# Weight conversion, preparation and batch order of a two-stage attention and SoLU kernel re-planned

## The chip, the core and the metric

The kernel runs on one core of one Trainium2 chip. The metric is the device time of one execution in microseconds (us); lower is better. The core has five engines that run side by side, each through its own instructions in order: TensorE (PE in the rows, its weight loads PEld), VectorE (DVE), ScalarE (ACT), GpSimd (POOL) and SyncE (SP), which here issues every DMA.

## The reference, cut to what matters

```python
def _attn_ref(q, k, v, p):                 # q,k,v: (8, 8, 576, 64), p: (8, 8, 32, 64)
    def sm_attn(qq, kk, vv):
        s = scale * np.matmul(qq, kk.transpose(0, 1, 3, 2))
        s = s - np.max(s, axis=-1, keepdims=True)
        a = np.exp(s)
        a = a / (np.sum(a, axis=-1, keepdims=True) + 1e-09)
        return np.matmul(a, vv)
    p_packed = sm_attn(p, k, v)
    return sm_attn(q, p_packed, p_packed)

def _moe_ref(x, w_in, w_out, g_ln):        # x: 4608 x 512, w_in: 512 x 1024, w_out: 1024 x 512
    h = x @ w_in
    e = np.exp(h - np.max(h, axis=-1, keepdims=True))
    solu = h * e / (np.sum(e, axis=-1, keepdims=True) + 1e-09)
    mu = np.mean(solu, axis=-1, keepdims=True)
    var = np.mean((solu - mu) ** 2, axis=-1, keepdims=True)
    ln = (solu - mu) / np.sqrt(var + 1e-06) * g_ln
    return ln @ w_out
```

The attention's output, with batch and sequence as rows, is `x`. The three weights come in as 64-bit floats; everything else is 32-bit.

## The kernel before

**Preparation (batch 0 and the weights).** `w_in` and `w_out` arrive as pairs of 32-bit words in four chunks each, which one string, `LOADS`, puts between the loads of k, v, q and p. A chunk is converted in two steps: `high_part` (ACT L202, DVE L204 and L205) builds the upper bits, and `add_low_part` adds the lower word. The string `HOW` says for each of the eight chunks which engines do that second step: the lower word is scaled by ACT (L220) or inside one DVE instruction (L217), multiplied by DVE or GpSimd (L221), and added by DVE or GpSimd (L233) or by two matmuls and an ACT copy (L226, L227). For `w_out` there follow the column sums on TensorE (L302), one scale (L307 to L311), and for each of eight half chunks a multiplication by that scale (L322, `SCALED_BY`), a rounding to 16 bits `wch` (ACT L323) and the rest `wcl` (L330, `REST_BY`). `ZL_BY` and `A2L_BY` do the same for two tensors of batch 0.

**The attention of a batch b** is two generators. `pack(b)`: transposes of k (DVE L350), scores of p in two groups of matmuls (L368; L360 for batch 0), their maximum (L371, L373) and exponent (ACT L381), transposes (L397), the product with v (L407), `pp` (DVE L411) and its transpose (L413, L415). `unpack(b)`: transposes of q (L428), scores in two groups (L467), each read by DVE (L439), a softmax (DVE L443, GpSimd L444, ACT L446, DVE L448 to L450, GpSimd L451), `zh` and `zl`, the product of `w_in` with the packed values in two groups (matmuls L483, then ACT L485 and DVE L500), and `a2h` and `a2l` (L505, L507, L508). L368, L467, L483, L397 and L407 write the same two PSUM banks `pa`, so a group of 16 matmuls starts when VectorE or ScalarE has read both banks of the group before.

**The MLP** takes 36 tiles of 128 rows, called tile 0 to 35 here. `mlp_in`: 12 matmuls of 512 columns into `h` (L521; 24 for a tile that two batches share), the row maximum (DVE L523), exponent (ACT L531), the product `u` (DVE L534). `mlp_norm`: GpSimd's small `negmu` (L542), `yhl` in two halves (ACT L544, DVE L545), and one transposing DMA `yT` (L547, on SP's queue). `mlp_out`: 24 matmuls into `po` (L564), then DVE's `o_sb` (L566) and the store.

**What sets the order.** A scheduler places the instructions of each engine by priorities. The numbers in `PACK0`, `W_IN`, `UNPACK0`, `W_OUT`, `SCALE_AT`, `CHUNKS`, `PARTS` are priority offsets for the preparation; `FIRST_BATCH` and `LATER` say after which tile a step of `unpack(b + 1)` and of `pack(b + 2)` is written. From batch 1 on TensorE's order is that of the code. `BUSY` adds matmuls on constants that nothing reads (L255). SP takes its DMAs in one order, with at most eight under way.

## Time and profile before

| what | us |
|---|---|
| median of three runs | 471.25 (470.44 to 472.5) |
| the profiled execution's own time | 472.61 |
| its span, first to last instruction | 470.8 |
| TensorE busy in it | 430.8 (92%) |
| VectorE busy | 350.5 (74%) |
| ScalarE busy | 232.3 (49%) |
| GpSimd busy | 147.1 (31%) |

Times inside the profile count from the start of the span; the profiled execution is 1.8 us longer than its span, and 1.36 us above the median of the runs. The first output matmul (L564) starts at 108.85 us and the last ends with the span.

### The profile page before, as it was taken

The numbers are of one execution on the slowest core, as the hardware profiler recorded it, in microseconds if no ns is written. First come the engines' busy times: TensorE is split into PE (matmuls) and PEld (weight loads), VectorE is DVE, ScalarE is ACT, GpSimd is POOL, SyncE is SP. The second block draws the span as 40 slices with busy tenths as digits, with TensorE's granted clock in tenths as the row PEclk, the third lists the DMA queues.
The fourth block names the chain that finished last, engine by engine and source line by source line (L and its number), as shares of the span: only waits on it lengthen the run. The fifth ranks groups of instructions, "written<-read, shape, count | busy, mean of one in ns | idle before, by whom it ended". The sixth has DMA issues, their size and how long they took to land.

```text
span 470.8 us, 8265 instructions
## 1 busy us (share of the span) xinstructions
PE 430.8 (92%) x3116; PEld 234.4 (50%) x3116; DVE 350.5 (74%) x648; ACT 232.3 (49%) x404; POOL 147.1 (31%) x244
## 2 busy tenths in 40 slices
...
GB/s 257 338 274 290 149 205 118 130 208 148 104 151 173 165 120 202 159 140 137 220 71 165 98 206 101 98 100 173 51 84 68 92 45 90 112 67 130 73 101 77
DMA packets 237880, 67.00 MB, mean 142 GB/s; under 512 B 208912, under 2 KB 231440, under 8 KB 237328
## 3 DMA queue, kind: packets, MB, share of 16 engines
...
q8 instruction: 24, 0.39, 0.4%
...
## 4 chain that ended last, share of the span: by engine, by line
PE 42%; DVE 28%; POOL 7%; ACT 6%; issue 6%; DMA 6%; SPq 5%; DVEq 0%; ACTq 0%; POOLq 0%
PE po L564 21%; PE h L521 12%; DVE nm L523 4%; DMA zh<-in_moe_w_in_dram 3%; DVE u L534 3%; DVE qT L428 3%; DVE kT L350 3%; PE pa L407 3%; DVE yhl L545 2%; DVE zl L500 2%; ACT yhl L544 2%; SPq L134 2%; DMA raw<-in_k_dram 2%; ACT e L381 1%; DVE a2l L508 1%
## 5 line engine op out<-in xcount | busy, mean ns | idle before, releaser
L564 PE MATMUL po<-wch,yT 128*128 128x512 f16 x576 | 178.2, 380 | 1.2 <-DMA yT<-yhl 1.2
L564 PEld LDWEIGHTS <-yT 128*128 128x128 f16 x864 | 80.9, 98 | 113.0 <-issue 18.4
L564 PE MATMUL po<-wcl,yT 128*128 128x512 f16 x288 | 108.7, 379 | 0.0
L521 PE MATMUL h<-zh,a2h 128*128 128x512 f32 x160 | 69.3, 433 | 1.7 <-DVE u L534 1.7
L531 ACT ACTIVATE e<-h,nm 128x1024 f32<-128x1024 f32 x36 | 39.9, 1109 | 59.4 <-DVE nm L523 59.4
L544 ACT ACTIVATE yhl<-u,negmu 128x1024 f16<-128x1024 f32 x36 | 41.4, 1149 | 49.7 <-POOL negmu L542 49.2
L521 PE MATMUL h<-zh,a2l 128*128 128x512 f32 x160 | 64.6, 404 | 0.3 <-DVE a2l L508 0.3
L521 PE MATMUL h<-zl,a2h 128*128 128x512 f32 x160 | 63.9, 400 | 0.6 <-POOL zl L493 0.6
L523 DVE TENSOR_REDUCE nm<-h 128x1 f32<-128x1024 f32 x36 | 43.9, 1220 | 23.6 <-PE h L521 23.5
L545 DVE SCALAR_TENSOR_TENSOR yhl<-u,negmu,yhl 128x1024 f16<-128x1024 f32 x36 | 46.4, 1288 | 17.5 <-ACT yhl L544 17.3
L534 DVE SCALAR_TENSOR_TENSOR u<-e,s_row,h 128x1024 f32<-128x1024 f32 x36 | 45.6, 1267 | 8.6 <-ACT e L531 7.4
L551 POOL TENSOR_SCALAR s_eps<-se,s_row 128x1 f32<-128x1 f32 x36 | 10.8, 301 | 121.7 <-ACT e L531 80.5
L566 DVE SCALAR_TENSOR_TENSOR o_sb<-po,c_row,inv 128x512 f32<-128x512 f32 x36 | 26.6, 738 | 22.6 <-PE po L564 22.6
L549 ACT ACTIVATE e<-u,negmu 128x1024 f32<-128x1024 f32 x36 | 40.9, 1137 | 3.4 <-POOL negmu L542 3.4
L554 POOL TENSOR_SCALAR c_row<-sq,s_eps 128x1 f32<-128x1 f32 x36 | 17.7, 492 | 79.4 <-ACT e L549 79.3
L521 PEld LDWEIGHTS h<-zh,a2h 128*128 128x128 f32 x160 | 31.0, 193 | 16.5 <-issue 7.9
L521 PEld LDWEIGHTS h<-zh,a2l 128*128 128x128 f32 x160 | 30.8, 192 | 9.0 <-DVE a2l L508 1.3
L521 PEld LDWEIGHTS h<-zl,a2h 128*128 128x128 f32 x160 | 30.8, 193 | 7.1 <-POOL zl L493 0.9
L485 ACT CAST zh<-pa 128x512 fp32r<-128x512 f32 x28 | 15.1, 583 | 26.1 <-PE pa L483 26.1
L444 POOL TENSOR_TENSOR s<-s,mx 128x576 f32<-128x576 f32 x14 | 15.9, 1158 | 36.9 <-DVE mx L443 36.9
L381 ACT ACTIVATE e<-pa,nmx 128x288 f32<-128x288 f32 x28 | 13.8, 497 | 26.9 <-DVE nmx L373 26.9
L483 PE MATMUL pa<-w_in_sb,ppT 64*32 64x512 f32 x224 | 19.9, 631 | 2.6 <-DVE zl L500 2.6
...
## 6 DMA issues: line engine op xcount, KB each, us to landing
...
```

Source lines behind the costliest of these rows:

```text
L381: nc.scalar.activation(dst, src, AF.Exp, bias=nmx, accum_out=es[:, n:n + 1])
L483: nc.tensor.matmul(banks[r][32 * g:32 * g + 32, :], lhsT=ppT[rows, 32 * g:32 * g + 32], rhs=w_in_sb[rows, g, cols], start=True, stop=True)
L521: nc.tensor.matmul(h[:, 512 * n:512 * n + 512], lhsT=lhsT, rhs=z[:, r, 512 * n:512 * n + 512], start=t == 0, stop=t == len(terms) - 1)
L523: nc.vector.tensor_reduce(out=nm, in_=h, axis=AX.X, op=ALU.max, negate=True)
L531: nc.scalar.activation(e, h, AF.Exp, bias=nm, accum_out=se)
L534: nc.vector.scalar_tensor_tensor(out=u, in0=e, scalar=s_row, in1=h, op0=ALU.mult, op1=ALU.mult, accum_out=su)
L544: nc.scalar.activation(yhl[:, 0], u, AF.Identity, bias=negmu)
L545: nc.vector.scalar_tensor_tensor(out=yhl[:, 1], in0=u, scalar=negmu, in1=yhl[:, 0], op0=ALU.add, op1=ALU.subtract)
L549: nc.scalar.activation(e, u, AF.Square, bias=negmu, accum_out=sq)
L554: nc.gpsimd.tensor_scalar(out=c_row, in0=sq, scalar1=1.0 / DF, scalar2=s_eps, op0=ALU.mult, op1=ALU.add)
L564: nc.tensor.matmul(po, lhsT=yT[:, a, c], rhs=w[:, c], start=c == 0 and t == 0, stop=c == NFC - 1 and t == 2)
L566: nc.vector.scalar_tensor_tensor(out=o_sb, in0=po, scalar=c_row, in1=inv, op0=ALU.mult, op1=ALU.mult)
```

## The change

Five strings move parts of the conversion. `HOW`: the first chunk of `w_in` loses both its GpSimd instructions to VectorE; the first of `w_out` loses an ACT and a GpSimd instruction to one of VectorE; the last of `w_out` moves its addition from GpSimd to VectorE. `SCALED_BY`: one half chunk goes from GpSimd to VectorE, two more from ACT and GpSimd to one fused VectorE instruction each. `REST_BY`: two go from GpSimd to VectorE, one the other way. `ZL_BY`: one of four goes to VectorE, which reads PSUM, without the ACT copy. `A2L_BY`: one of two goes from VectorE to GpSimd. `BUSY` drops from 22 to 6 matmuls. All priority offsets and both tables of batch orders have other numbers, and `LOADS` other places for k and one w. The two new strings `YT_BY` and `STORE_BY` are all 's', which leaves the DMAs on SP.

```diff
-HOW = '14313324'
-SCALED_BY = 'pppppdpp'
-REST_BY = 'pdddppdd'
-ZL_BY = 'pppp'
-A2L_BY = 'dd'
-PACK0 = [-350, 400, 2010, 365, -1000, 60, -2800, 200, 200]
...
-LOADS = 'wpkwvwwqooPoo'
-BUSY = [[8, 100], [6, 0], [0, -3000], [0, -100], [2, -190], [0, -485], [4, 200], [2, -2885], [28, 285], [134, -20], [26, 20], [64, 50]]
...
+HOW = '54316325'
+SCALED_BY = 'pppdpdss'
+REST_BY = 'pdddddpd'
+ZL_BY = 'pppd'
+A2L_BY = 'pd'
+PACK0 = [1025, -200, 100, 100, -160, -75, -75, 80, -50]
...
+LOADS = 'wkpwwvwqoooPo'
...
+BUSY = [[0, -3025], [0, -3000], [6, -400], [0, 850], [0, -20], [0, -10], [0, 100], [0, 400]]
+YT_BY = 'ssssssssss'
+STORE_BY = 's'
...
-        nc.sync.dma_start(yT.rearrange('p t c n -> p (t c) n'), yhl.rearrange('p t f -> p (t f)'), transpose=True)
+        queue = nc.scalar if YT_BY[min(row // P, 9)] == 'a' else nc.sync
+        queue.dma_start(yT.rearrange('p t c n -> p (t c) n'), yhl.rearrange('p t f -> p (t f)'), transpose=True)
...
-            nc.sync.dma_start(*stores.pop(0))
+            (nc.scalar if STORE_BY == 'a' else nc.sync).dma_start(*stores.pop(0))
```

Line numbers of the changed kernel are two to three higher (L523 for L521, L567 for L564). A row that is followed by "..." stands for itself and its like up to the next row shown.

**Place 1, the first batch.** SP's queue around the first transposes, before:

```order
L85 DMA raw_684<-in_q_dram 32x18x32 x16
L96 DMA raw_1353<-in_k_dram 32x72x32 x4
L85 DMA raw_1362<-in_q_dram 32x18x32 x11
L107 DMA v_sb_680<-in_v_dram 128x8x128 x2
L134 DMA v_sb_680<-in_v_dram 64x8x64
L547 DMA_TRANSPOSE yT_971<-yhl_968 128x16x128
L547 DMA_TRANSPOSE yT_1135<-yhl_1132 128x16x128
L85 DMA raw_1362<-in_q_dram 32x18x32 x5
L96 DMA raw_1860<-in_k_dram 32x72x32 x4
L547 DMA_TRANSPOSE yT_1225<-yhl_1222 128x16x128
```

and changed:

```order
L87 DMA raw_669<-in_q_dram 32x18x32 x16
L98 DMA raw_1332<-in_k_dram 32x72x32 x4
L87 DMA raw_1341<-in_q_dram 32x18x32 x11
L550 DMA_TRANSPOSE yT_1036<-yhl_1033 128x16x128
L109 DMA v_sb_665<-in_v_dram 128x8x128 x2
L136 DMA v_sb_665<-in_v_dram 64x8x64
L87 DMA raw_1341<-in_q_dram 32x18x32 x3
L550 DMA_TRANSPOSE yT_1085<-yhl_1082 128x16x128
L87 DMA raw_1341<-in_q_dram 32x18x32 x2
L550 DMA_TRANSPOSE yT_1204<-yhl_1201 128x16x128
```

The same loads stand ahead of the first transpose, except that the three DMAs of batch 2's v now follow it; the second and third transposes are spread between the q loads. TensorE at the same place, before (h_1174 is tile 3, h_1270 the shared tile 4, po_1145 and po_1236 the outputs of tiles 0 and 1, pa_896 to pa_935 batch 1's scores, pa_983 batch 1's first group of L483):

```order
L521 MATMUL h_1174<-zh_500,a2h0_182 128x512
...
L467 MATMUL pa_896<-qT_845,ppT_843 32x288
...
L467 MATMUL pa_934<-qT_845,ppT_843 32x288 x4
L467 MATMUL pa_935<-qT_845,ppT_843 32x288 x4
L521 MATMUL h_1270<-zh_500,a2h0_182 128x512
...
L483 MATMUL pa_983<-w_in_sb_126,ppT_843 32x512 x4
L483 MATMUL pa_984<-w_in_sb_126,ppT_843 32x512 x4
L564 MATMUL po_1145<-wch_127,yT_971 128x512
```

and changed (pa_832 is batch 2's first L368 group, h_1153 tile 3, h_1249 tile 4, po_1095, po_1215, po_1303 the outputs of tiles 0 to 2, pa_902 and pa_914 batch 1's scores, pa_948 to pa_963 its L483, pa_976 batch 2's second L368 group):

```order
L370 MATMUL pa_832<-kT_712,pT2_84 32x288 x4
L523 MATMUL h_1153<-zh_486,a2h0_182 128x512
...
L567 MATMUL po_1095<-wch_127,yT_1036 128x512
...
L523 MATMUL h_1249<-zh_486,a2h0_182 128x512
...
L469 MATMUL pa_902<-qT_851,ppT_828 32x288
...
L567 MATMUL po_1215<-wch_127,yT_1085 128x512
...
L469 MATMUL pa_914<-qT_851,ppT_828 32x288
...
L567 MATMUL po_1303<-wch_127,yT_1204 128x512
...
L485 MATMUL pa_948<-w_in_sb_126,ppT_828 32x512 x4
...
L485 MATMUL pa_962<-w_in_sb_126,ppT_828 32x512 x4
L523 MATMUL h_1249<-zh_946,a2h1_186 128x512
...
L370 MATMUL pa_976<-kT_712,pT2_84 32x288 x4
```

Batch 1's scores moved from ahead of the first output matmul to behind 15 of it, and the outputs of tiles 0 to 2 all stand ahead of batch 1's second L483 group; before, the third output stood behind it.

**Place 2, an even batch (batch 2; batches 4 and 6 are alike, 6 without L368).** TensorE before: pa_1893 scores, h_1937 and h_2036 tiles 9 and 10, pa_1965 and pa_2008 the two L483 groups, pa_2069 and pa_2135 the two L368 groups.

```order
L467 MATMUL pa_1893<-qT_1886,ppT_1841 32x288
...
L521 MATMUL h_1937<-zh_1456,a2h0_182 128x512
...
L483 MATMUL pa_1965<-w_in_sb_126,ppT_1841 32x512
...
L564 MATMUL po_1995<-wch_127,yT_1808 128x512
...
L483 MATMUL pa_2008<-w_in_sb_126,ppT_1841 32x512
...
L521 MATMUL h_2036<-zh_1456,a2h0_182 128x512
...
L368 MATMUL pa_2069<-kT_2062,pT2_84 32x288
...
L564 MATMUL po_2104<-wch_127,yT_1984 128x512
...
L368 MATMUL pa_2135<-kT_2062,pT2_84 32x288
```

and changed (h_1916, h_2001, h_2110 tiles 9 to 11; pa_1944 and pa_2061 L483's groups; pa_2091 and pa_2136 L368's):

```order
L523 MATMUL h_1916<-zh_1409,a2h0_182 128x512
...
L485 MATMUL pa_1944<-w_in_sb_126,ppT_1820 32x512
...
L567 MATMUL po_1974<-wch_127,yT_1787 128x512
...
L523 MATMUL h_2001<-zh_1409,a2h0_182 128x512
...
L567 MATMUL po_2048<-wch_127,yT_1963 128x512
...
L485 MATMUL pa_2061<-w_in_sb_126,ppT_1820 32x512
...
L370 MATMUL pa_2091<-kT_2027,pT2_84 32x288
...
L523 MATMUL h_2110<-zh_1409,a2h0_182 128x512
...
L370 MATMUL pa_2136<-kT_2027,pT2_84 32x288
```

Between the two L483 groups there were 12 output matmuls, now 36 and a tile; between the second of them and the first L368 group there were 12 and a tile, now 12 alone; between the two L368 groups there were 24, now one tile (12 matmuls of L521).

**Place 3, an odd batch (batch 3; 5 is alike).** TensorE before: pa_2553 and pa_2610 L483's groups, h_2624 tile 15, po_2675 the output ahead of L368's first group pa_2690, h_2723 tile 16.

```order
L483 MATMUL pa_2553<-w_in_sb_126,ppT_2348 32x512
...
L564 MATMUL po_2583<-wch_127,yT_2407 128x512
...
L483 MATMUL pa_2610<-w_in_sb_126,ppT_2348 32x512
...
L521 MATMUL h_2624<-zh_1963,a2h1_186 128x512
...
L564 MATMUL po_2675<-wch_127,yT_2572 128x512
...
L368 MATMUL pa_2690<-kT_2654,pT2_84 32x288
```

and changed (h_2520 and h_2608 tiles 14 and 15):

```order
L485 MATMUL pa_2506<-w_in_sb_126,ppT_2327 32x512
...
L523 MATMUL h_2520<-zh_1942,a2h1_186 128x512
...
L485 MATMUL pa_2580<-w_in_sb_126,ppT_2327 32x512
...
L567 MATMUL po_2567<-wch_127,yT_2386 128x512
...
L523 MATMUL h_2608<-zh_1942,a2h1_186 128x512
...
L370 MATMUL pa_2636<-kT_2546,pT2_84 32x288
```

Tile 14 moved between the two L483 groups; the distance from the second to L368 is still one tile and 12 output matmuls. Batch 1 has the same new order as batch 3, but at its start the first L483 group stands directly behind the scores, ahead of tile 5; before, tile 5 stood between them.

## Rows read from the trace of the kernel before

**Rows 1.** The page: span, and busy time and instructions of each engine.

```profile
span 470.8 us, 8265 instructions
PE 430.8 (92%) x3116; PEld 234.4 (50%) x3116; DVE 350.5 (74%) x648; ACT 232.3 (49%) x404; POOL 147.1 (31%) x244
```

**Rows 2.** Busy time of the engines in stretches (from:to, length, busy of PE, PEld, DVE, ACT, POOL, granted clock, DMA share, GB/s); the first is a stretch of the preparation, the last row sums nine stretches from 57 to 467 us.

```profile
20.00:70.00 50.00, 39.32 (x290) 19.55 (x290) 40.70 (x61) 33.69 (x60) 24.14 (x11) 0.81 1.13 240
57.00:109.00 52.00, 38.81 (x298) 22.14 (x298) 42.87 (x74) 30.50 (x59) 32.88 (x34) 0.80 1.08 168
109.00:142.00 33.00, 29.90 (x261) 13.81 (x259) 23.73 (x48) 14.01 (x27) 8.53 (x12) 1.00 0.77 129
...
sum 410.00, PE 385.07 PEld 206.26 DVE 311.79 ACT 195.83 POOL 123.32; mean PE 42.79 PEld 22.92 DVE 34.64 ACT 21.76 POOL 13.70
```

**Rows 3.** Timeline of SP's DMA queue, preparation and first batch (start, duration of the issue, what).

```profile
70.69 11.66 SPq L85 DMA_DIRECT2D raw<-in_q_dram  x16
82.48 6.18 SPq L96 DMA_DIRECT2D raw<-in_k_dram  x4
89.19 8.45 SPq L85 DMA_DIRECT2D raw<-in_q_dram  x11
97.74 1.07 SPq L107 DMA_DIRECT2D v_sb<-in_v_dram  x2
...
100.13 5.83 SPq L547 DMA_TRANSPOSE yT<-yhl  x2
...
117.52 3.23 SPq L547 DMA_TRANSPOSE yT<-yhl  x1
```

**Rows 4.** DMA issues in the stretch 100.2 to 100.3: the first transpose, us from issue to landing.

```profile
yT<-yhl SPq DMA_TRANSPOSE x1, 6.0
```

**Rows 5.** Timeline of TensorE around the first output matmul (start, duration, what, in brackets the idle time before and what ended it).

```profile
96.96 0.72 PE L467 MATMUL pa<-qT,ppT 64*32 64x288 f32 x16
102.40 1.55 PE L467 MATMUL pa<-qT,ppT 64*32 64x288 f32 x16 [4.71 <-DVE s L439]
...
108.85 0.39 PE L564 MATMUL po<-wch,yT 128*128 128x512 f16 x1
```

**Rows 6.** Timeline of VectorE: the second half of tile 0's yhl, and of batch 1's unpack the last a2l.

```profile
90.27 1.29 DVE L545 SCALAR_TENSOR_TENSOR yhl<-u,negmu,yhl 128x1024 f16<-128x1024 f32 x1 [1.56 <-ACT yhl L544]
...
120.47 0.74 DVE L508 TENSOR_TENSOR a2l<-s,a2h 128x576 fp32r<-128x576 f32 x1
```

**Rows 7.** Timeline of TensorE, from pack(2)'s transposes to batch 2's first L483 group.

```profile
134.34 1.58 PE L397 MATMUL pa<-ident,e 128*128 128x128 f32 x8 [1.03 <-ACT e L381]
...
141.06 1.08 PE L467 MATMUL pa<-qT,ppT 64*32 64x288 f32 x16 [0.62 <-DVE s L439]
...
145.06 1.09 PE L483 MATMUL pa<-w_in_sb,ppT 64*32 64x512 f32 x16
```

**Rows 8.** Timeline of TensorE, groups of L483 and L368 in the later batches.

```profile
152.32 1.04 PE L483 MATMUL pa<-w_in_sb,ppT 64*32 64x512 f32 x2 [0.89 <-DVE zl L500]
153.58 1.09 PE L483 MATMUL pa<-w_in_sb,ppT 64*32 64x512 f32 x14 [0.22 <-DVE zl L500]
...
166.70 1.19 PE L368 MATMUL pa<-kT,pT 64*32 64x288 f32 x16 [0.40 <-ACT e L381]
...
193.30 1.68 PE L483 MATMUL pa<-w_in_sb,ppT 64*32 64x512 f32 x16
...
206.31 0.72 PE L368 MATMUL pa<-kT,pT 64*32 64x288 f32 x16
...
254.43 0.67 PE L368 MATMUL pa<-kT,pT 64*32 64x288 f32 x2
255.94 0.71 PE L368 MATMUL pa<-kT,pT 64*32 64x288 f32 x14 [0.84 <-DVE zl L500]
...
384.56 1.69 PE L483 MATMUL pa<-w_in_sb,ppT 64*32 64x512 f32 x16 [1.45 <-DVE zl L500]
```

**Rows 9.** Timeline of TensorE, VectorE and ScalarE in batch 2, from its first L368 group to the tile behind the second.

```profile
200.38 0.72 PE L368 MATMUL pa<-kT,pT 64*32 64x288 f32 x16
...
203.71 0.82 DVE L371 TENSOR_REDUCE mx<-pa 128x1 f32<-128x288 f32 x2
...
205.69 0.20 ACT L381 ACTIVATION_READ_ACCUMULATOR e<-pa,nmx 128x1 f32 x1
...
206.95 0.50 PE L521 MATMUL h<-zh,a2h 128*128 128x512 f32 x1
...
209.81 0.39 PE L564 MATMUL po<-wch,yT 128*128 128x512 f16 x1
```

**Rows 10.** GpSimd's groups up to 110 us (busy, mean ns), conversion lines.

```profile
L221 POOL TENSOR_TENSOR u<-u 128x1024 fp32r<-128x1024 f32 (+1 forms) x5 | 13.0, 2604 | 27.6 <-ACT u L220 17.2 <-DVE u L212 10.4
L322 POOL TENSOR_TENSOR yhl<-yhl,o_sb 128x512 f32<-128x512 f32 x4 | 6.4, 1629 | 0.1
```

**Rows 11.** Timelines of GpSimd and VectorE in the preparation.

```profile
18.94 1.22 DVE L221 TENSOR_TENSOR u<-u 128x1024 f32<-128x1024 f32 x1 [1.02 <-ACT u L220]
...
42.65 2.75 POOL L233 TENSOR_TENSOR w_in_sb<-w_in_sb,u 128x1024 f32<-128x1024 f32 x1
43.12 2.84 DVE L204 TENSOR_SCALAR e<-e 128x1024 int32<-128x1024 int32 x1
...
77.25 1.76 DVE L322 TENSOR_TENSOR yT<-yT,o_sb 128x512 f32<-128x512 f32 x1
```

16 lines of the change are left out of this document (8 added, 8 removed).

## The prediction

> **What bounds the kernel now.** I read the page's span and busy times first: TensorE is busy 430.8 of 470.8 us, 92% [rows 1]. A share over the whole span hides where the idle 40 us lie, so the next view was the busy time by stretches. The sum from 57 to 467 us leaves TensorE idle for 410.00 - 385.07 = 24.9 us. Of these 52.00 - 38.81 = 13.2 lie between 57 and 109, so only 11.7 lie in the 358 us after the first output matmul [rows 2]. From 109 us on TensorE is the bound, and a better order can win 11.7 us there at the very most, 2.5% of the time. Before 109 it waits for something else: VectorE, ScalarE and GpSimd are all partly idle there too, and the clock granted to TensorE is 0.80 of full [rows 2].
>
> The timeline of SP's queue tells what. Its DMA issues for q, k, q and v follow one another from 70.69 us to 98.8 with next to no gap: 70.69 + 11.66 = 82.35, then 82.48 + 6.18 = 88.66, then 89.19 + 8.45 = 97.64 [rows 3]. The first transpose (L547) is issued at 100.13, though the second half of its input, yhl, was ready at 90.27 + 1.29 = 91.56 [rows 6]. It lands 6.0 us after its issue [rows 4], about 106.1, and the first output matmul starts at 108.85 [rows 5]. So the preparation is bound by the stream of DMAs, not by the engines that convert weights. While it waits, TensorE has batch 1's scores, whose second group waits 4.71 us for VectorE; the first group ran in 0.72 us at 96.96, the second, the same 16 matmuls, in 1.55 at 102.40 [rows 5].
>
> In the later batches I measured each wait by the group of matmuls that holds it, as the time from the group's start to its end, idle time before it included, less what an undisturbed group takes: 1.09 us for L483 [rows 7], 0.72 for L368 at 206.31 [rows 8]. By that batch 1 loses 153.58 + 1.09 - 152.32 + 0.89 - 1.09 = 2.15 at L483 and 0.40 + 1.19 - 0.72 = 0.87 at L368; batch 2 loses 1.68 - 1.09 = 0.59 at L483; batch 3 loses 255.94 + 0.71 - 254.43 - 0.72 = 1.50 at L368; batch 6 loses 1.45 + 1.69 - 1.09 = 2.05 at L483 [rows 8]. I take batch 4 as 2 and batch 5 as 3.
>
> **The conversion.** GpSimd loses two L221 of 2.60 us [rows 10], two L233 of up to 2.75 [rows 11], four L322 or L330 of 1.63 [rows 10] and one L493 of the same width, and takes one a2l: some 17 us less by these rows. VectorE takes four instructions of 1024 columns at 1.22 us [rows 11], five of 512 at about 0.66 (the a2l of 576 columns takes 0.74 [rows 6], 0.74 x 512 / 576 = 0.66), and gives one a2l of 0.74: 4.9 + 3.3 - 0.7 = 7.4 us more. ScalarE gives some 3 us. I cost all of it at nothing. The cover is SP's stream, which the conversion does not feed; VectorE is idle for 50.00 - 40.70 = 9.3 us from 20 to 70 [rows 2], so 7.4 fit. Without the cover it could cost what does not fit. Upper bound: if VectorE's moved instructions all meet GpSimd as L322 did at 77.25, in 1.76 instead of 0.66 [rows 11], the nine cost 9.9 us more, 17.3 in all, of which 8.0 do not fit.
>
> Rows 11 show what such a meeting is: L204 took 2.84 us at 43.12, in the shadow of a GpSimd instruction that ran from 42.65 to 45.40, and ended 0.56 behind it. The Trainium skill, page "SBUF — State Buffer", section "Who interferes with whom", says why: VectorE and GpSimd share a pair of ports as an exclusive lock, a VectorE instruction with two SBUF inputs needs it too, and the order of issue decides who waits. The trace agrees with both cases. The rule speaks against the change, since the moved instructions have two SBUF inputs each; by it the term is up to the 8.0 us and not 0.
>
> The 16 fewer dummy matmuls I cost at 0, because TensorE waits for the stream there; if its clock fell in the gap, the cost would be some of what lies before 57 us, all ahead of the same stream.
>
> **The first batch.** The first transpose now stands ahead of v's three DMAs, so it issues at about 97.7, when the q loads are through, 2.4 earlier, and lands about 103.7. The output matmuls of tile 0 start there. But the shared tile 4 and batch 1's scores now stand behind 15 of them. An output matmul takes (206.31 - 201.10) / 24 = 0.217 us, one of a tile's twelve (209.81 - 206.95) / 12 = 0.238 [rows 8, 9]; 15 and 6 make 4.7 us at full clock, 9.4 at half, so the scores start at 108.4 to 113.1, and I take 109.5, 12.5 later than the 96.96 of before. From there to the last a2l it was 120.47 + 0.74 - 96.96 = 24.3 us [rows 5, 6]. The same again would end at 133.8; tile 4's rest and the transposes of pack(2) (L397) stand behind it, which gives L397 at about 136.5. On the other side, TensorE has the same work to do by L397 as before, and it idled 33.00 - 29.90 = 3.1 us from 109 to 142 [rows 2]. If no wait is left, L397 starts at 134.34 - 3.1 = 131.2. Before it was 134.34 [rows 7]. So the term is -3.1 to +2.2; I take 0, since the 24.3 hold the 4.71 us wait that need not return.
>
> Behind that, batch 1's first L483 group stands directly behind the scores instead of behind a tile. It waits for L439 to read both banks: a wait for one L439 was 0.62 [rows 7], so 0 to 1.3; I take 1.0, because nothing stands between. pp (L411) may queue behind a yhl half of 1.29 on VectorE [rows 6]: 0 to 1.3, I take 0.5.
>
> **The later batches.** In odd batches tile 14 moves between the two L483 groups. VectorE gets a tile's 2.9 us more to read the first group, so zl is through before L368: -1.5 in batch 3 and in batch 5. Batch 1 has the same order: -2.15 - 0.87 = -3.0. But its L368 group can wait for the exponent of the one before: from the maximum's start to the exponent's end are 205.89 - 203.71 = 2.18 us [rows 9], so 0 to 2.1, half taken, 1.05. In batch 6, 36 matmuls and a tile stand between the L483 groups where 12 stood: -2.05. Batches 2 and 4 get the same, -0.59 each. What is late next is their L368: the first group stands only 12 output matmuls (2.6 us) behind L483, the second only one tile (2.86) behind the first. The distance of 2.6 + 2.9 = 5.5 that the first had sufficed in batch 2, so it can be late by 0 to 2.9. For the second the nearest link is 201.10 to 205.89 = 4.8 us [rows 9], with other work of VectorE in it, and 2.18 at least: 0 to 1.9. I take 1.4 together for each of the two batches, 2.8, nearer the low ends, since VectorE has a tile less to do there. The tail keeps its order: 0.
>
> Sum: 0 + 1.0 + 0.5 - 3.0 + 1.05 - 1.2 + 2.8 - 3.0 - 2.05 = -3.9. The profiled execution's own time is 472.61 and becomes 468.7; it stood 1.36 above the median, 471.25, so against the median I forecast 467.3, 0.8% less.
>
> **The rivals.** (a) *The waits only move.* Each wait of TensorE for VectorE is a queue's, and VectorE's work after 109 is unchanged, so what is taken from L483 comes back at L368, as it could by the 2.9 and 1.9 us above: up to 2 x 4.8 = 9.6 against gains of 9.2. At the middle of that (4.8 for both batches, and the full 2.1 in batch 1) the sum is near -0.9, the time 470 to 471.5. For it: batch 3 loses at L368 although its L483 lost nothing [rows 8]. Against it: gaps of a tile remove real queueing.
> (b) *Slower: batch 1's unpack comes too late.* If the 24.3 us chain repeats whole and starts at half clock, from 113.1, the last a2l ends at 137.4 and L397 starts at about 140, +5.7; with half the later gains that ends at 474 to 476. It decides when that a2l ends later than about 130. For it: the start is 12.5 us later; against it: 72 output matmuls stand ready as cover.
> (c) *Slower by the ports.* The conversion's 8.0 us reach q's loads, whose start at 70.69 waits for buffers that VectorE frees, and all later work shifts: 467.3 + 8.0 = 475.3, and it decides from 6.3 on, where the time passes 473.6. For it: the 2.84 and 1.76 of rows 11. Against it: 17 us of GpSimd's instructions are gone, so meetings are fewer.
> (d) *Better:* the first batch becomes bound by work, 3.1 less, and L368 costs nothing in batches 2 and 4: 461 to 464.
>
> **How the numbers follow.** Forecast 0.40 (465 to 469), (a) 0.27, (b) 0.18, (c) 0.06, (d) 0.09. A measurement of this kernel tells about 0.5% from no change. Faster is forecast and (d), 0.49; same is (a), 0.27; slower (b) and (c), 0.24. The range leaves out the lower end of (d) and the upper of (b): 461.5 to 475. The likeliest case's own range is 465 to 469.
>
> **What would show it.** The first transpose issued near 97.7 and landing near 103.7; the first output matmul about 104 and L397 at 131 to 136.5; no idle time at L483 in batches 1, 2, 4 and 6, none at L368 in 3 and 5, and less than 2 us at L368 in 2 and 4. SP's q loads still at 70.7 and unbroken would show the conversion hidden. I am wrong if those loads start 2 us later or earlier, since then the stream was fed by the conversion after all, or if TensorE's idle time after 109 stays near 11.7.

## The result and the profile after

The changed kernel takes 473.75 us (median of 10 runs, 472.11 to 476.3) against 472.13 before (10 runs): a ratio of 1.0051, 95% interval 1.0029 to 1.0074. It is a little slower; I had forecast 0.8% faster. Run once more it gave 474.16 us and 1.0050 (1.0029 to 1.0072).

The page of the profiled execution after; its own time is 476.3 us:

```profile
span 474.5 us, 8233 instructions
PE 427.3 (90%) x3100; PEld 232.8 (49%) x3100; DVE 357.9 (75%) x656; ACT 228.4 (48%) x400; POOL 135.3 (29%) x236
```

VectorE is busy 7.4 us more than in [rows 1] and GpSimd 11.8 less: the conversion moved in the direction that the diff says. SP's queue at the first transposes, to be read against [rows 3] (start, duration of the issue, what):

```profile
72.01 11.13 SPq L87 DMA_DIRECT2D raw<-in_q_dram  x16
83.27 6.29 SPq L98 DMA_DIRECT2D raw<-in_k_dram  x4
90.09 8.54 SPq L87 DMA_DIRECT2D raw<-in_q_dram  x11
98.73 2.06 SPq L550 DMA_TRANSPOSE yT<-yhl  x1
```

The stream is as unbroken as before, and the first transpose goes out 1.4 us sooner. The busy time by stretches (as [rows 2]; the last two rows lie in the new trouble):

```profile
57.00:109.00 52.00, 38.83 (x278) 23.24 (x279) 44.79 (x77) 31.00 (x63) 29.08 (x30) 0.80 1.27 170
109.00:142.00 33.00, 27.83 (x258) 12.80 (x264) 24.53 (x48) 12.86 (x23) 6.93 (x11) 1.00 0.87 135
125.00:140.00 15.00, 11.33 (x144) 6.44 (x142) 12.47 (x25) 8.16 (x16) 2.45 (x5) 1.00 0.98 120
141.10:152.70 11.60, 9.96 (x61) 4.66 (x61) 8.23 (x16) 2.44 (x4) 2.63 (x3) 0.56 1.11 200
```

The same kind of rows of before, for the same two places:

```profile
125.00:140.00 15.00, 12.52 (x153) 6.47 (x156) 10.22 (x23) 6.00 (x12) 1.53 (x5) 1.00 0.59 124
140.00:152.00 12.00, 10.81 (x84) 4.94 (x68) 10.33 (x21) 3.75 (x7) 4.14 (x6) 1.00 0.92 167
```

From 109 to 142 us TensorE idles 5.2 us instead of 3.1, and from 141 to 153 it works hard, but at a granted clock of 0.56 (0.50, called half clock here, is the lower of its two levels); before, the clock was full there. The timeline of TensorE in between shows the waits (in brackets the idle time before and what ended it):

```profile
103.22 0.39 PE L567 MATMUL po<-wch,yT 128*128 128x512 f16 x1 [2.35 <-DMA yT<-yhl]
...
109.64 0.72 PE L469 MATMUL pa<-qT,ppT 64*32 64x288 f32 x16
...
128.52 0.50 PE L523 MATMUL h<-zh,a2h 128*128 128x512 f32 x1 [1.28 <-ACT a2h L509]
...
134.80 1.59 PE L399 MATMUL pa<-ident,e 128*128 128x128 f32 x8 [0.83 <-ACT e L383]
137.01 0.41 PE L399 MATMUL pa<-ident,e 128*64 128x128 f32 x2 [0.62 <-ACT e1T L400]
...
141.11 0.30 PE L415 MATMUL pa<-ident,pp 128*128 128x128 f32 x1 [1.89 <-DVE pp L413]
141.80 1.22 PE L469 MATMUL pa<-qT,ppT 64*32 64x288 f32 x16 [0.38 <-DVE ppT L417]
143.63 1.57 PE L469 MATMUL pa<-qT,ppT 64*32 64x288 f32 x16 [0.62 <-DVE s L441]
145.82 2.32 PE L485 MATMUL pa<-w_in_sb,ppT 64*32 64x512 f32 x16 [0.62 <-DVE s L441]
148.07 0.79 PE L523 MATMUL h<-zh,a2h 128*128 128x512 f32 x1
...
152.76 0.39 PE L567 MATMUL po<-wch,yT 128*128 128x512 f16 x1
```

Before, behind the first row of [rows 7]:

```profile
136.12 0.41 PE L397 MATMUL pa<-ident,e 128*64 128x128 f32 x2 [0.20 <-ACT e1T L398]
...
139.03 0.30 PE L413 MATMUL pa<-ident,pp 128*128 128x128 f32 x1 [0.69 <-DVE pp L411]
139.72 0.72 PE L467 MATMUL pa<-qT,ppT 64*32 64x288 f32 x16 [0.38 <-DVE ppT L415]
...
146.08 0.39 PE L564 MATMUL po<-wch,yT 128*128 128x512 f16 x1
```

(e1T is ScalarE's copy of the transposed exponent, ppT VectorE's of the transposed pp.) An L485 group now lasts 2.32 us where it took 1.09 [rows 7]. Tile 5's twelve matmuls fill 148.07 to 152.76, 4.7 us; before, from the end of the scores to L483, 2.9.

All kernels of this study have, but for the dummies of fill and fill2, the same work between two of pack's groups of transposes (L397, L399 after), so the starts of these groups cut the trace into comparable sections. Each number below is the difference of two such starts in one profiled execution; the first is the start of the first output matmul, the last runs to the end of the span. A section is named after the batch whose tiles lie in it; the attention in it is that of later batches. In batch 1's section the scores and the L485 groups are those of `unpack(2)` and the L370 groups those of `pack(3)`; some texts below call them batch 1's.

| kernel | first output | to pack(2) | to pack(3) | to pack(4) | to pack(5) | to pack(6) | to pack(7) | to the end |
|---|---|---|---|---|---|---|---|---|
| tiles of batch | | 0 | 1 | 2 | 3 | 4 | 5 | 6, 7 |
| before | 108.85 | 25.49 | 38.68 | 41.98 | 52.89 | 42.22 | 52.83 | 107.86 |
| changed | 103.22 | 31.58 | 41.66 | 43.35 | 51.83 | 46.16 | 50.98 | 105.72 |
| changed, again | 103.56 | 31.56 | 40.39 | 43.62 | 52.90 | 43.78 | 50.98 | 105.81 |
| conv_only | 102.14 | 43.47 | 43.21 | 42.26 | 52.86 | 42.23 | 52.90 | 107.93 |
| later_only | 106.12 | 26.16 | 38.99 | 43.36 | 53.35 | 44.03 | 50.98 | 105.81 |
| later_back | 102.81 | 32.08 | 42.42 | 41.99 | 52.87 | 42.21 | 52.92 | 108.00 |
| l485_behind | 101.97 | 30.87 | 44.43 | 43.36 | 51.89 | 43.70 | 50.98 | 106.00 |
| norm_first | 103.52 | 32.64 | 41.68 | 43.35 | 51.65 | 43.62 | 50.98 | 105.76 |
| fill | 103.53 | 31.58 | 44.47 | 44.14 | 53.50 | 43.64 | 50.99 | 105.75 |
| fill2 | 102.32 | 31.34 | 41.27 | 43.35 | 55.31 | 43.74 | 50.98 | 105.89 |
| pp_first | 104.62 | 32.24 | 41.48 | 43.51 | 51.64 | 43.98 | 50.98 | 105.75 |
| ppt_first | 103.98 | 31.99 | 40.88 | 43.36 | 51.92 | 44.13 | 50.98 | 105.76 |
| yhl_last | 103.31 | 31.58 | 42.03 | 43.63 | 51.98 | 43.74 | 50.98 | 105.75 |
| kt_later | 103.03 | 31.32 | 40.13 | 43.36 | 51.85 | 46.00 | 50.98 | 105.83 |
| scores_early | 102.81 | 41.99 | 43.77 | 43.65 | 51.71 | 43.97 | 50.98 | 105.72 |
| scores_early_even | 102.67 | 42.48 | 43.89 | 42.77 | 52.43 | 42.74 | 51.83 | 105.79 |
| even_back_pp | 103.52 | 31.43 | 42.81 | 42.63 | 52.37 | 42.82 | 51.81 | 105.81 |
| mixed | 107.40 | 26.03 | 39.07 | 42.46 | 52.36 | 43.15 | 51.47 | 105.76 |
| mixed_kt | 107.62 | 24.78 | 38.66 | 42.42 | 52.38 | 42.79 | 51.82 | 105.73 |

The first output matmul starts between 102.0 and 104.6 us in kernels with the changed preparation, between 106.1 and 108.9 with before's, so single executions differ by 2 us there; the sections of batches 5 and 6 repeat within 0.3 us for one order.

### The profile page after: what moved, and what is told of

It is laid out like the page before. It is cut to its first block, busy times and chain, and to the rows that moved or that the text cites. A ratio compares the mean times of both kernels' runs of the same rounds, so it can differ in the third digit from the quotient of the medians.

```text
span 474.5 us, 8233 instructions
## 1 busy us (share of the span) xinstructions
PE 427.3 (90%) x3100; PEld 232.8 (49%) x3100; DVE 357.9 (75%) x656; ACT 228.4 (48%) x400; POOL 135.3 (29%) x236
## 4 chain that ended last, share of the span: by engine, by line
PE 61%; DVE 19%; DMA 11%; SPq 3%; issue 3%; ACT 2%; POOL 0%; DVEq 0%; ACTq 0%
PE po L567 33%; PE h L523 19%; DMA yT<-yhl 3%; DMA raw<-in_k_dram 3%; DMA raw<-in_moe_w_out_dram 2%; PE pa L485 2%; DVE kT L352 2%; PE pa L409 2%; PE pa L469 2%; DMA zl<-in_moe_w_in_dram 2%; DVE yhl L547 2%; DVE u L536 2%; DVE nm L525 2%; PE pa L370 1%; PE pa L399 1%
## 5 line engine op out<-in xcount | busy, mean ns | idle before, releaser
L567 PE MATMUL po<-wch,yT 128*128 128x512 f16 x576 | 181.5, 385 | 5.6 <-DMA yT<-yhl 5.6
L567 PEld LDWEIGHTS <-yT 128*128 128x128 f16 x864 | 81.7, 99 | 119.4 <-issue 20.6
L567 PE MATMUL po<-wcl,yT 128*128 128x512 f16 x288 | 110.5, 384 | 0.0
L523 PE MATMUL h<-zh,a2h 128*128 128x512 f32 x160 | 70.5, 441 | 6.1 <-ACT a2h L509 3.6
L533 ACT ACTIVATE e<-h,nm 128x1024 f32<-128x1024 f32 x36 | 40.1, 1113 | 70.3 <-DVE nm L525 70.3
L523 PE MATMUL h<-zh,a2l 128*128 128x512 f32 x160 | 65.3, 408 | 0.2 <-DVE a2l L510 0.2
L523 PE MATMUL h<-zl,a2h 128*128 128x512 f32 x160 | 64.9, 406 | 0.0
L547 DVE SCALAR_TENSOR_TENSOR yhl<-u,negmu,yhl 128x1024 f16<-128x1024 f32 x36 | 47.9, 1332 | 16.3 <-ACT yhl L546 16.2
L557 POOL TENSOR_SCALAR c_row<-sq,s_eps 128x1 f32<-128x1 f32 x36 | 19.1, 532 | 86.6 <-ACT e L552 86.6
L523 PEld LDWEIGHTS h<-zh,a2h 128*128 128x128 f32 x160 | 31.5, 197 | 22.2 <-issue 6.6
L523 PEld LDWEIGHTS h<-zh,a2l 128*128 128x128 f32 x160 | 31.3, 196 | 9.3 <-DVE a2l L510 1.1
L523 PEld LDWEIGHTS h<-zl,a2h 128*128 128x128 f32 x160 | 31.5, 197 | 6.4 <-DVE zl L490 0.3
L446 POOL TENSOR_TENSOR s<-s,mx 128x576 f32<-128x576 f32 x14 | 16.0, 1158 | 31.3 <-DVE mx L445 31.3
L441 DVE STREAM_TRANSPOSE s<-pa 128x288 f32<-128x288 f32 x28 | 11.9, 462 | 13.7 <-PE pa L469 13.7
```

Source lines behind the costliest of these rows:

```text
L446: eng.tensor_tensor(out=s2[r], in0=s2[r], in1=mx.unsqueeze(2).broadcast_to([P, NB, J]), op=ALU.subtract)
L523: nc.tensor.matmul(h[:, 512 * n:512 * n + 512], lhsT=lhsT, rhs=z[:, r, 512 * n:512 * n + 512], start=t == 0, stop=t == len(terms) - 1)
L533: nc.scalar.activation(e, h, AF.Exp, bias=nm, accum_out=se)
L547: nc.vector.scalar_tensor_tensor(out=yhl[:, 1], in0=u, scalar=negmu, in1=yhl[:, 0], op0=ALU.add, op1=ALU.subtract)
L557: nc.gpsimd.tensor_scalar(out=c_row, in0=sq, scalar1=1.0 / DF, scalar2=s_eps, op0=ALU.mult, op1=ALU.add)
L567: nc.tensor.matmul(po, lhsT=yT[:, a, c], rhs=w[:, c], start=c == 0 and t == 0, stop=c == NFC - 1 and t == 2)
```

## Experiments

### One half of the change at a time

conv_only, the kernel before with the five conversion strings:

```diff
-HOW = '14313324'
+HOW = '54316325'
-SCALED_BY = 'pppppdpp'
+SCALED_BY = 'pppdpdss'
...
```

> The kernel before with the five conversion strings of the change alone; order tables, priority offsets, loads and dummies as before. Theory (the conversion hides behind SP's stream of loads, the loss is in the later order): same time as before within 0.3%, q's loads at 70.7 us start within 1 us of that. Rival (VectorE and GpSimd meet, the stream starts late): q's loads start 2 us later or more, and the time is 0.5 to 1.7% longer.

488.64 us, ratio 1.0363 (1.0338 to 1.0388). The stream was on time, q's loads at 71.28 us, so neither side had the mechanism. TensorE's timeline (same columns as above):

```profile
115.58 0.71 PE L467 MATMUL pa<-qT,ppT 64*32 64x288 f32 x16
...
127.98 2.52 PE L483 MATMUL pa<-w_in_sb,ppT 64*32 64x512 f32 x16 [4.13 <-DVE zl L500]
...
145.61 2.71 PE L397 MATMUL pa<-ident,e 128*128 128x128 f32 x10 [4.85 <-ACT e L381]
```

Eight instructions more on VectorE (656 against 648) make the scheduler place the whole first batch in another order under the old priorities: batch 1's scores run at 115.6 instead of 97 us, and pack(2) at 145.6. The other priorities of the change are therefore no part that could be left out; conversion and first batch are taken as one piece from here on. The reverse, before's conversion under the change's priorities, was not run.

later_only (before, with the change's `LATER`) and later_back (the change, with before's `LATER`) cut it into the two pieces that do come apart:

> The kernel before with the change's LATER table alone. Theory (the loss is in LATER, by L483 ahead of tile 5 and by transposes late in SP's queue): batch 1's first L483 group costs 1 to 6 us and batch 4 up to 4, against 8 us won at other groups, so between 1% faster and 0.5% slower, with the same rows as in the changed kernel at L483 and L368. Rival (the loss comes from the first batch, whose tile 4 ends just ahead of L397 and fills VectorE and ScalarE there): no loss at batch 1's first L483 group beyond 1 us, and the time is about 0.9% shorter.

> The changed kernel with the LATER table of before. Theory (first batch and conversion cost 0.5 us, L397 at 134.8): the time of before within 0.3%, and the waits of before at L483 and L368 are back. Rival (the first batch's order is what costs): TensorE still waits near 1.9 us for pp and runs at half clock behind L397, and the time stays 0.5% longer or more.

later_only: 471.37 us, ratio 0.9998 (0.9980 to 1.0015). later_back: 477.16 us, 1.0112 (1.0092 to 1.0133). later_only's theory held: the time lies in its range, batch 1's first L483 group brings a loss of some 3.6 us (below), batch 4's section takes 1.8 more, and batches 5 and 6 win 1.9 and 2.1. So `LATER` wins nothing under before's first batch, and 3 us under the changed one. later_back's theory fell; the piece of preparation and first batch costs: with before's `LATER` it takes 5.5 us by the medians, and in its profile 0.55 up to pack(2) and 3.7 in the next section (42.42 against 38.68). Its rival held: TensorE waits 1.89 us for pp there too, and the clock is at half behind it.

### Batch 1's section

l485_behind moves the first L485 group of that section behind tile 5:

```diff
-ui = [4, 0, 1, 0, ...]
+ui = [3, 1, 1, 0, ...]     # loop of batch 1 alone
```

> The changed kernel with batch 1's first L483 group (L485 here) written behind tile 5 instead of ahead of it, as before; nothing else. Theory (that place lets TensorE idle, and the idle time drops its clock to half for the next 11 us): the stretch from L399 to the end of tile 5 and that group, 18.0 us in the changed kernel, shrinks by 2 to 5 us, and the time by as much, to 0.2 to 0.6% under before. Rival (the clock falls already from the 1.9 us wait for pp ahead of it): it shrinks by less than 1.5 us, and the granted clock in it stays near 0.56.

476.95 us, 1.0127 (1.0097 to 1.0157), and the section grew to 44.43. The theory fell. The stretch that it named, 18.0 us in the changed kernel, took 16.65, so it shrank by 1.3 as the rival allowed. TensorE's clock was at 0.50 from 140 to 145 us all the same, and the second L485 group waited again, as before the change. Over the whole section the place ahead of tile 5 is the better one in the changed kernel.

What that place costs by itself is read from later_only, where the first batch is before's. The section is cut at the start of its scores and where tile 5 and the first L483 group are both done (us, one profile each):

| kernel | first batch | first L483 group | to the scores | to the end of both | rest |
|---|---|---|---|---|---|
| before | before's | behind tile 5 | 5.38 | 6.36 | 26.94 |
| mixed (below) | before's | behind tile 5 | 5.37 | 7.91 | 25.79 |
| later_only | before's | ahead of it | 5.38 | 9.93 | 23.68 |
| later_back | changed | behind tile 5 | 8.13 | 9.20 | 25.09 |
| l485_behind | changed | behind tile 5 | 8.13 | 8.52 | 27.78 |
| changed | changed | ahead of it | 7.00 | 10.96 | 23.70 |
| changed, again | changed | ahead of it | 6.95 | 9.38 | 24.06 |

In later_only the middle part is 3.57 us longer than before. The new wait is 0.57 of it; the rest comes with the half clock, at which the L483 group takes 2.25 us to the next start and tile 5 4.25:

```profile
141.09 2.32 PE L483 MATMUL pa<-w_in_sb,ppT 64*32 64x512 f32 x16 [0.57 <-DVE s L439]
143.34 0.79 PE L521 MATMUL h<-zh,a2h 128*128 128x512 f32 x1
...
147.59 0.39 PE L564 MATMUL po<-wch,yT 128*128 128x512 f16 x1
```

```profile
140.00:145.00 5.00, 4.43 (x30) 1.77 (x21) 4.45 (x8) 1.07 (x2) 0.25 (x1) 0.50 1.06 249
```

So the half clock does not need the changed first batch: the new place of this group is followed by it too, and with the changed first batch it comes at either place. What only the changed first batch brings, of these seven, is the 1.6 to 2.8 us more ahead of the scores. mixed has before's order in this section and yet 0.66 granted from 140 to 145, so single executions differ by some 1.5 us here.

The next three take tile 4's work, which now ends just ahead of pack(2)'s steps, from in front of them on VectorE. pp_first makes the second half of tile 4's yhl wait for pp, ppt_first for ppT, yhl_last for the transposes of the scores (L441):

```diff
+late = 0 * pp[:, 1, :1] + negmu                      # VectorE; ppT or the scores in the other two
-yhl[:, 1] = (u + negmu) - yhl[:, 0]
+yhl[:, 1] = (u + late) - yhl[:, 0]
```

> The changed kernel with one order turned on VectorE: pack(2)'s pp (L413) ahead of the second half of tile 4's yhl (L547), by a one-column instruction that makes yhl wait for pp; every other engine's order is the same. Theory (tile 4 ends just ahead of pack(2)'s last steps, its work on VectorE stands in front of pp, and the gap that this makes on TensorE brings the half clock): TensorE's wait for pp falls from 1.9 to about 0.7 us, and the section from pack(2)'s L399 to pack(3)'s shrinks by 1.2 us by the wait alone and by up to 3 with the clock, to 38.5 to 40 us. Rival (tile 4's work only changes place; the scores' transposes on VectorE set the pace): the section stays within 0.5 us of 40.4 to 41.7.

> As the run with pp ahead of yhl, with the second half of tile 4's yhl behind the copy of ppT as well; the other engines' orders are the changed kernel's. In the run with pp alone, the wait for pp fell by 1.2 us and the wait for ppT grew by 1.1, since yhl now stood ahead of that copy. Theory: both waits are short now, batch 1's scores start 1.2 us earlier after pack(2)'s L399 (5.8 instead of 7.0 us), and the section from pack(2)'s L399 to pack(3)'s shrinks by 1 to 3 us from 40.4 to 41.7. Rival: yhl now delays the transposes of the scores (L441), and the section stays.

> As the run above, with the second half of tile 4's yhl behind all the transposes of batch 1's scores, so that nothing of tile 4 stands on VectorE from pp to there. Theory: the section from pack(2)'s L399 to pack(3)'s falls to 38 to 39.5 us, near before's 38.7 to 39.1, and the time by 1 to 3 us against the changed kernel. Rival (ScalarE's copies behind tile 4's exponent, and the idle time ahead of L399, are enough to bring the half clock): the section stays above 40 us.

pp_first 474.6 us (1.0057, 1.0031 to 1.0082), ppt_first 473.24 (1.0017, 1.0000 to 1.0034), yhl_last 474.49 (1.0038, 1.0018 to 1.0058). In pp_first the wait only moved one instruction on, from pp to ppT:

```profile
141.96 0.30 PE L415 MATMUL pa<-ident,pp 128*128 128x128 f32 x1 [0.69 <-DVE pp L413]
143.72 1.22 PE L469 MATMUL pa<-qT,ppT 64*32 64x288 f32 x16 [1.46 <-DVE ppT L417]
```

In yhl_last both waits are short, and still the scores start 7.01 us behind L399 and the section takes 42.03 us: the clock falls already in L409, and an L486 group (L485 of the changed kernel) lasts 2.32 us, since the granted clock is at half:

```profile
141.07 0.45 PE L415 MATMUL pa<-ident,pp 128*128 128x128 f32 x1 [0.69 <-DVE pp L413]
141.90 1.22 PE L469 MATMUL pa<-qT,ppT 64*32 64x288 f32 x16 [0.38 <-DVE ppT L417]
...
145.93 2.32 PE L486 MATMUL pa<-w_in_sb,ppT 64*32 64x512 f32 x16 [0.62 <-DVE s L441]
```

```profile
138.00:151.00 13.00, 10.69 (x128) 5.09 (x121) 7.22 (x16) 3.57 (x6) 2.37 (x5) 0.50 0.93 168
```

So a shorter queue on VectorE behind L399 does not bring the clock back. ppt_first is the only one that may have won something, about 0.3%, at the edge of what its interval tells.

kt_later goes one step further up: pack(3)'s four k transposes (L352, 2.75 us) stand on VectorE between pack(2)'s maximum and nmx, before the change and after it; here they wait for nmx.

```diff
+kT[:, :, 0] = 0 * nmx of pack(2)                     # pack(3), ahead of its four transposes
```

> The changed kernel with pack(3)'s four k transposes (L352, 2.75 us on VectorE) put behind pack(2)'s nmx (L375) by a four-element write that they must wait for; in the changed kernel, and in before, they stand between pack(2)'s maximum and nmx, and nmx frees the exponent that L399 waits for. The scheduler then also places tile 4's exponent on ScalarE behind the e1T copies and its yhl behind ppT; TensorE's order is the changed kernel's. Theory (from batch 1's last a2l on, at 130.9 us, L399 follows VectorE's queue, and tile 4 collides with pack(2)): L399 comes up to 2.5 us sooner after the first output matmul (29 to 30 us instead of 31.6), less where tile 4's matmuls, which end at 134.0, are in its way (then 30.8); the section behind it shrinks by 1 us or more, and the time by 1 to 3 us. Rival (the half clock follows the idle time, wherever it stands): L399 comes sooner and the section behind it grows by as much.

474.0 us, 1.0035 (1.0018 to 1.0052). L399's wait of 0.83 us is gone, but tile 4's second half, behind its 1.28 us wait for a2h, ends only at 134.35; L399 starts 31.3 us behind the first output matmul, as in the changed kernel, and the clock is low on both sides of it (0.75 granted from 130 to 135 us, 0.50 from 140 to 145). What pp_first to kt_later have in common lies above L399: tile 4 waits for batch 1's a2h. As I read the trace, that is because batch 1's scores run at 109.6 and 115.1 us and not at 97 and 102.4 [rows 5], and the output matmuls of tiles 0 to 2, which lay beside that chain before, are used up ahead of it. No run shows that this brings the half clock: in later_only the same scores run at 94.81 and 100.26 us, and the clock falls in the section all the same.

scores_early was meant to put those scores back (`FIRST_BATCH`, first list: 0, 0, 5 becomes 0, 3, 2), and scores_early_even added before's even row:

> The changed kernel with one list of FIRST_BATCH other ([0, 0, 5, 0, ...] becomes [0, 3, 2, 0, ...]): batch 1's scores stand directly behind pack(1)'s ppT and behind tile 3, ahead of the first output matmul, as in before; preparation, conversion, LATER as in the change. Theory (batch 1's unpack starts 13 us late in the changed kernel, the output matmuls that could cover its chain are used up ahead of it, and from 125 us on TensorE waits and falls to half clock): the scores run near 97 us, batch 1's a2h is in time, the section from the first output matmul to pack(2)'s L399 shrinks by 1 to 3 us or the next one by 2, the clock stays full from 135 to 150 us, and the time is 2 to 5 us shorter, 469 to 472. Rival (the half clock comes from pack(2)'s own chain, exponent to pp): both sections stay within 1 us, and the time stays near 474.

> As the run above, with before's row of LATER for batches 2 and 4 besides. Theory: the sections of batches 2 and 4 are 0.7 to 1.3 us shorter each, batch 5's 0.8 longer, as in the run with that row before; 1 us less in sum. Rival: no difference.

488.48 us (1.0345, 1.0319 to 1.0372) and 487.58 (1.0336, 1.0312 to 1.0361). They decide nothing: the scores ran at 95.3 and 99.7, but the scheduler also put k's four loads ahead of two transposes in SP's queue; an output matmul waited 4.35 us for yT and L399 5.41 us for its exponent.

### The clock

fill and fill2 put dummy matmuls, which nothing reads, where TensorE waits in batch 1's section: ten (six) behind pack(2)'s L409 in unused columns of its bank, and six in a bank of the scores (three in a free bank) behind each group of scores.

> The changed kernel with 22 short dummy matmuls into unused columns of pa where TensorE waits ahead of batch 1: ten behind pack(2)'s L409, six behind each group of batch 1's scores (1.6 and 0.6 us of work at full clock). They compute nothing that is read. Theory (the half clock from 141 to 153 us is what idle TensorE brings, and it costs 3 to 4 of the 6.2 us lost there): the clock stays at full, and the section from pack(2)'s L399 to pack(3)'s shrinks from 41.7 to between 37.5 and 39.5, the time by 0.4 to 0.9%. Rival (the engines ahead are late, the clock follows): the section shrinks by less than 1 us, or grows by the dummies' time.

> As the run with 22 dummies, but fewer, and no longer in the banks that VectorE reads: six of 384 columns behind pack(2)'s L409, and three of 512 columns into a free po bank behind each group of batch 1's scores. Theory (clock): the granted clock stays at full from 135 to 155 us, tile 5's 12 matmuls take near 2.9 us instead of 4.7, and the section from pack(2)'s L399 to pack(3)'s takes 38 to 39.5 us instead of 40.4 to 41.7. Rival: the clock falls all the same, or the section does not shrink although the clock stays.

fill: 479.46 us, 1.0160 (1.0127 to 1.0192); fill2: 474.18, 1.0039 (1.0008 to 1.0069). Dummies in a bank wait for its reader, or it for them: in fill the six behind each group of scores stand 0.98 us for L441, and the group behind them with them, so its section grew by 3 us although the clock stayed full until 145. In fill2 pp stands 0.88 us for the six ahead of it, but behind the scores the clock is back (0.50 from 140 to 145 us, 0.91 from 145 to 150):

```profile
139.00 2.27 PE L411 MATMUL pa<-ones 128*128 128x384 f32 x6
141.93 0.45 PE L415 MATMUL pa<-ident,pp 128*128 128x128 f32 x1 [0.66 <-DVE pp L413]
...
147.19 1.27 PE L485 MATMUL pa<-w_in_sb,ppT 64*32 64x512 f32 x16
148.38 0.50 PE L523 MATMUL h<-zh,a2h 128*128 128x512 f32 x1
```

The L485 group and tile 5 take 1.2 and 2.9 us to the next start, where the changed kernel takes 2.25 and 4.69, 2.9 us more (in its second profile 2.25 and 3.33, 1.5 more). That is the price of the half clock in these two steps, measured at either level. The section as a whole, 41.27 us, won nothing: from L399 to the scores it took 9.10 us instead of 7.00. Half of that arose ahead of the dummies, where TensorE stood 2.09 us for ScalarE's e1T, and the rest at the dummies and behind them. So the price of the half clock is measured, but no run took it away and kept the rest.

### The later batches

after_again is the changed kernel once more; norm_first puts `mlp_norm` back to offset 1000 in `LATER`, which changes SP's queue alone: in the loops of batches 2 and 4 a transpose stands ahead of v's loads instead of behind them and q's.

> The changed kernel once more, for a second profile. If batch 4's 3.9 us more than before belong to this order of instructions, the section from L399 of pack(5) to that of pack(6) takes 46 us again; if they are an accident of one execution (its transposing DMA landed 0.04 us before the matmul that waited 2.1 us for it), it takes near 43.7, as in the two other kernels with the same LATER table. Batch 1's section stays at 41.7 and batches 5 and 6 at 51.0 and 105.8.

> The changed kernel with the priority offset of mlp_norm in LATER at 1000 as before; only SP's queue differs: in loops 2 and 4 a transpose stands ahead of v's loads instead of behind them. Theory (transposes behind v and q are a cost of the change in even batches): sections of batches 2 and 4 shrink by 0 to 2.2 us each, batch 4 more than batch 2, and the time by 0.2 to 0.6%. Rival (TensorE waits there for VectorE's readers of pa, L483 and L368, and the transposes are in time): same time within 0.2%.

after_again: 474.16 us (1.0050, 1.0029 to 1.0072), batch 4's section 43.78. So 2.4 us of the first profile's 46.16 were that execution's own. Its transpose was 2.09 us late, and the granted clock behind it was 0.70 (290 to 295 us); in the second profile the same wait was 1.39 us and the clock 1.00:

```profile
291.72 0.39 PE L567 MATMUL po<-wch,yT 128*128 128x512 f16 x1 [2.09 <-DMA yT<-yhl]
```

```profile
291.41 0.39 PE L567 MATMUL po<-wch,yT 128*128 128x512 f16 x1 [1.39 <-DMA yT<-yhl]
```

The transpose of that stretch is not late in one execution alone: in all eleven profiles with the change's row for batches 2 and 4 and its offset of `mlp_norm`, TensorE waits 1.1 to 2.1 us for a transpose in batch 2's or batch 4's section, and in four of them also in batch 3's (in after_again 1.10 us at 237.74, in fill2 1.97, in a section of 55.31). norm_first: 473.89 us, 1.0043 (1.0026 to 1.0059): against 1.0050 no difference that can be told. Its transposes in these two sections are in time, but L370 waits 0.90 and 0.93 us there for VectorE's zl, and the sections keep their length (43.35 and 43.62): the wait only changes its place.

mixed takes from the change only the rows of `LATER` for the loops of batches 3, 5 and 6; mixed_kt adds the order of kt_later; even_back_pp is the changed kernel with before's row for 2 and 4 and with pp first.

```diff
-LATER[(b - 1) % 2]
+(NEW_LATER if b in (3, 5, 6) else LATER)[(b - 1) % 2]
```

> The kernel before, with the change's rows of LATER for the loops of batches 3, 5 and 6 alone. Theory (the change's orders win 1 to 1.9 us each in batches 3 and 5 and 2.1 in batch 6, and lose in 1, 2 and 4): sections of batches 3 and 5 near 51 to 52 instead of 52.9, the last 105.8 instead of 107.9, all others as before, so 4 to 5.8 us in all, 0.8 to 1.2% faster than before. Rival (what is won moves to the next batch): less than 0.4% faster.

> The changed kernel with before's row of LATER for the loops of batches 2 and 4, and with pp ahead of yhl as in the run above. Theory (the change's even order costs 1.5 us in each of batches 2 and 4 by L370 right behind L485, and wins 2.1 in batch 6): their sections return to 42.0 to 42.5, the last stays at 105.8, and the time is 3 us shorter than that of the run above, 467 to 470. Rival (the sections are tied to the odd batches' order before them): less than 1 us shorter.

> The kernel before with the change's orders in batches 3, 5 and 6 (469.2 us), and pack(3)'s k transposes behind pack(2)'s nmx as in the run above. Theory: L397 comes up to 2.5 us sooner, the section behind it stays at 38.7 to 39.1 us, and the time is 466.5 to 468.5 us. Rival: what L397 wins comes back as waits or half clock behind it, 469 us again.

mixed: 469.23 us, 0.9942 (0.9927 to 0.9958), less than expected: batches 3 and 5 win 0.5 and 1.4, batch 6 its 2.1, but batches 2 and 4 lose 0.5 and 0.9, since a loop's steps run over into the next. even_back_pp: 473.89, 1.0039 (1.0019 to 1.0060): sections of 2 and 4 back to 42.6 and 42.8, near the 42.0 to 42.5 expected, but 5 gives 0.8 back and batch 1 takes 42.81. The time is 0.7 us under pp_first's, as its rival said. mixed_kt: 468.1 us, 0.9926 (0.9909 to 0.9944), faster than before and than the change, and within the expected range; from mixed its interval does not part it. There L398 (L397 of before) has no wait:

```profile
132.40 1.58 PE L398 MATMUL pa<-ident,e 128*128 128x128 f32 x8
134.18 0.41 PE L398 MATMUL pa<-ident,e 128*64 128x128 f32 x2 [0.20 <-ACT e1T L399]
```

It comes 24.78 us behind the first output matmul, 1.25 sooner than in mixed, with the clock full from 125 to 152 us. The order that gave the changed kernel nothing brings L398 forward where tile 4 is done before pack(2); that it shortens the time is not shown.

## Why the prediction was wrong, point by point

Measured values are those of the changed kernel's two profiles, as the sections against before; the second (474.34 us, near the median) stands last; its transpose in batch 4 is 1.39 us late, not 2.09. The sign that I had named for being wrong came: TensorE's idle time behind 109 us is 13.3 us (to 470.7) and 13.9 (to 468.8), where 11.7 stood before.

**The bound.** Right: SP's stream held, and the first transpose went out at 98.73 (forecast 97.7) and the first output matmul started at 103.22 (103.7). That the second fits better than the first is luck: q's loads started 1.3 us later, and the transpose landed 4.4 us after its issue, where I had 6.0.

**Conversion 0, and the ports.** In the changed kernel right, as far as the times tell: VectorE's busy time grew by 357.9 - 350.5 = 7.4 us, and the 17.3 of the port rival would show there. That 7.4 is also the uncontended sum is luck: later_only, with before's conversion, has 353.4 us, and later_back, with the changed one, 355.9. The Trainium skill, page "SBUF — State Buffer", section "Who interferes with whom", lets a VectorE instruction with two inputs in SBUF wait for a GpSimd instruction that reads SBUF; totals so far below 17.3 agree with meetings that cost no more in sum than before. (One of the nine moved instructions, a zl, reads PSUM, so "two SBUF inputs each" was wrong of it.) But "cost all of it at nothing" passed over that the scheduler re-sorts the first batch when the conversion moves, as conv_only shows with 17 us.

**The first batch's term, 0 (-3.1 to +2.2).** pack(2)'s transposes started at 134.80 and 135.12, against 134.34: +0.5 and +0.8. Right, in part by luck: the scores started at 109.64 (109.5), but the last a2l ended at 130.63 us (133.8), 3.2 earlier, and L399 stood 4.2 us behind it where I had 2.7:

```profile
129.22 1.41 DVE L510 TENSOR_TENSOR a2l<-s,a2h 128x576 fp32r<-128x576 f32 x2
...
131.28 2.75 DVE L352 STREAM_TRANSPOSE kT<-raw 128x576 f32<-128x576 f32 x4
133.95 0.12 DVE L375 TENSOR_REDUCE nmx<-mx 128x1 f32<-128x2 f32 x1
```

**Batch 1, forecast -3.0 + 1.05 + 1.0 + 0.5 = -0.45: the step that failed.** Measured +3.0 and +1.7, term by term from the table of the three parts:

- L483 directly behind the scores, forecast +1.0: measured +4.6 and +3.0, and +3.6 in later_only. The wait was 0.62 us, inside my 0 to 1.3. The rest is half clock: 2.9 and 1.5 us in the L485 group and tile 5, and 1.05 and 0.84 in the scores ahead of them. I had priced this place by its wait alone and counted half clock only ahead of 109 us, so this cost stood at nothing.
- pp behind a yhl half, forecast +0.5: measured +1.6 in both, 1.2 at pp and 0.4 at e1T. Tile 4, which I had seen move behind the output matmuls, does its exponent, u and yhl among pack(2)'s steps.
- L485's second group and L370 without a wait, forecast -3.0 + 1.05: measured -3.2 and -2.9. This mechanism was right, and the wait for the exponent did not come.

The waits of 0.4 to 1.9 us on TensorE (11.3 us busy of 15 from 125 to 140, 12.5 before) were followed by the half clock. before, later_only, mixed and mixed_kt, with before's first batch, have 38.7 to 39.1 in this section; the fifteen rows of the table with the changed preparation, or its conversion alone, have 40.1 to 44.5. Rival (b) had the late unpack, and its threshold of 130 us was passed by 0.6; it had the loss ahead of L397, where the runs have it behind, and later_only loses 3.57 us in the middle part without a late unpack.

**Batches 2 and 4, +0.81 each.** +1.4 and +1.6 in batch 2, +1.6 in batch 4 (second profile). The gain at L485 came. In the first profile's batch 2, L370 lost more than the 1.4 I took, inside the bounds:

```profile
204.72 1.09 PE L485 MATMUL pa<-w_in_sb,ppT 64*32 64x512 f32 x16
...
209.44 1.31 PE L370 MATMUL pa<-kT,pT 64*32 64x288 f32 x16 [0.94 <-DVE zl L502]
...
213.63 1.07 PE L370 MATMUL pa<-kT,pT 64*32 64x288 f32 x16
```

The first group loses 0.94 + 1.31 - 0.72 = 1.53, the second 0.35: 1.9. In the second profile L370 loses less, 0.73 in batch 2 and 0.59 in batch 4, but the output matmuls between the L485 groups wait 1.12 and 1.39 us for their transposes, a wait that I had at nothing. So, as rival (a) had it, part of what was taken from one wait came back at another.

**Batches 3 and 5, -1.5 each.** -1.1 and 0.0 in batch 3, -1.85 in batch 5. Both L370 groups of batch 3 run undisturbed:

```profile
256.39 0.71 PE L370 MATMUL pa<-kT,pT 64*32 64x288 f32 x16
...
265.09 0.71 PE L370 MATMUL pa<-kT,pT 64*32 64x288 f32 x16
```

In the second profile 1.10 of the gain went to the late transpose; I had looked at no transpose behind 120 us.

**Batch 6, -2.05.** -2.1 in both: right.

The second profile's sum: +0.8 + 1.7 + 1.6 + 0.0 + 1.6 - 1.85 - 2.05 = 1.8 us, against 1.6 between the medians. My -3.9 misses it by 5.7, of which 2.2 lie in batch 1, 1.5 in batch 3, 1.6 in batches 2 and 4 and 0.8 ahead of pack(2), less 0.35 in batch 5.

**What stays open.** That the clock, and not the waits alone, makes batch 1's section long is shown for two steps (1.5 to 2.9 us). What brings the clock down is not shown: from 125 to 140 us TensorE idles 3.7 us in the changed kernel and 3.1 in later_only, and half clock follows; it idles 3.0 in mixed, and the clock is lower for part of the next stretch; it idles 2.5 in before and 2.1 in mixed_kt, and the clock stays full. But in l485_behind a single wait of 2.71 us that ends at 154.96 leaves it full too (1.00 from 150 to 160 us). That the late scores of batch 1 make the idle time ahead of the scores of batch 2 is argued from the trace; the one run that undid it was spoilt by its DMA queue.
